# Attention and experts: normalizing the attention output in PSUM on VectorE, and all remainders on GpSimd

## The chip, the cores and the metric

The kernel runs on one core of a Trainium2 chip. TensorE (PE) does the matmuls into PSUM, VectorE (DVE), ScalarE (ACT) and GpSimd (POOL) do the elementwise work, and SyncE (SP) issues most of the DMAs. Each engine works through its own list of instructions in order and waits on semaphores for the others. The metric is the device time of one execution in microseconds (us); lower is better.

## The reference, cut to what matters

```python
scores = 1/sqrt(64) * q @ k.T                       # 8 batches, 8 heads, 576 positions, head size 64
bias   = minimum(-(cum[:, None] - cum[None, :]), 0) # cum = cumsum(maximum(s, 0))
scores = where(causal, -1e9, scores + bias)
attn   = exp(scores - max(scores))
attn   = attn / (sum(attn) + 1e-9)
x      = (attn @ v)                                 # heads side by side: 4608 tokens x 512
...
logits = x @ w_gate                                 # each of 8 experts takes 576 tokens
out[mask] = relu(x[mask] @ w1[e]) @ w2[e]
```

Matmuls are done in 16-bit pieces: a float32 number is the sum of a 16-bit "hi" piece and a "lo" piece, the remainder. So q, k, v, the exponentials P and the result x are each split, and the products of the pieces are added in PSUM.

## The kernel before

The program is one long hand-made schedule. Attention comes first, on 16 groups g of four heads (two groups make a batch); then come routing and the eight experts, which the change does not touch.

**The slots.** `run` (L600) walks through slots, 14 to a group; half a group (seven slots) belongs to one pair of heads, `pr`. In a slot the code first issues the slot's transposed score matmuls with their exponential (`st_units`, one unit a slot), then what earlier slots have posted (`post`, a number of slots later), then what the plan has for that slot. The table `T` (L39) holds the offsets. An engine's list is thus fixed by the order of the slots; nothing is moved at run time.

**The stages of one group.** Three groups are in flight at a time.

1. Preparation: `hi2` makes the hi pieces of q, k and v on ACT, `lo2` the lo pieces on DVE, two operations for each (L267). Behind each lo operation, and behind each row maximum, `pop` issues one more DVE operation from a list of waiting ones.
2. First pass (`spass_units`, L284): scores for the row maximum. Seven units to a half group, in the order one(0,3), one(0,2), comb, both(0), one(1,3), one(1,2), both(1). PE writes a bank `pss`, and one slot later DVE takes its maximum into `mr` (L297). The tag `pss` has three banks, and the small transpose `psm` (and the router's `psl` once a batch) takes its turn in the same three: because `psm` stands between one(1,3) and one(1,2), the bank of both(1) is the one that one(1,3) had, in the slot before.
3. Second pass (`st_units`, L374): transposed scores into `pst`, three banks; ACT takes the exponential into `P` (L391); the remainder `R` = P minus its upper 16 bits is a subtraction (L393) on POOL, or on DVE for the first block of each half and for the small last block (128 x 128).
4. Product with v (`pv_units`, L438): PE adds three products for each block into `po` (L457 to L459). The tag `po` has two banks, one for each `par`; a half group fills first par 0 and then par 1.
5. Normalizing (`norm`, L463): DVE adds a small number to the row sum (L470) and takes its reciprocal (L471). For three heads of four, five ACT operations then multiply out of PSUM into the float32 tile `xf` (L475), and for the fourth one DVE multiplication does (L479).
6. Pieces of x: `xh` (L484) makes the hi piece from `xf` on ACT in three operations a group, `xl` (L492) the lo piece on POOL in three operations. `xtr` and `xout` then transpose and store them by DMA, and `logits` (L510) multiplies them by the gate, 40 x 2 matmuls in slot 3 of every second group.

The last batch (groups 14 and 15) has its own ending, `tail` (L527).

Of the kernel before, what the change touches and what calls it, by code (L numbers as in the profile page):

```python
# [21 lines left out]
DM = 512  # L22
# [10 lines left out]
VS = 256.0  # L33
# [22 lines left out]
class Attention:  # L56
# [208 lines left out]
    def lo2(self, x, h, o, sc):  # L265
        def f(p):
            self.nc.vector.scalar_tensor_tensor(o[:, p], x[:, p], sc, h[:, p], op0=OP.mult, op1=OP.subtract)  # L267
            self.pop()
        return [lambda p=p: f(p) for p in range(2)]

    def vprep_units(self, g):
        st = self.st[g]
        V = self.pc.tile([128, 2, 9, 65], F16, name="V", bufs=3)
        Vl = self.pc.tile([128, 2, 9, 64], F16, name="Vl", bufs=3)
        st.update(V=V, Vl=Vl)
        return ([(0, lambda: self.nc.gpsimd.memset(V[:, :, :, 64:65], 1.0))] +
                list(zip(T["VHI"], self.hi2(st["rv"], V[:, :, :, 0:64], VS))) +
                list(zip(T["VLO"], self.lo2(st["rv"], V[:, :, :, 0:64], Vl, VS))))

    def q0(self, par, i):  # L280

# [92 lines left out]
    def st_units(self, g):  # L374

        nc, st = self.nc, self.st[g]
        Q, K = st["Q"], st["K"]
        units = []

        def mm(ps, c0, n, par, pr, ki, q0, diag=False):  # L380
            ks = slice(128 * ki, 128 * ki + 128)
            nc.tensor.matmul(ps[:, c0:c0 + n], K[0:70, 0, par, pr, ks], Q[0:70, 0, pr, par, q0:q0 + n],  # L382
                             start=True, stop=False)
            nc.tensor.matmul(ps[:, c0:c0 + n], K[:, 1, par, pr, ks], Q[:, 1, pr, par, q0:q0 + n],  # L384
                             start=False, stop=not diag)
            if diag:
                nc.tensor.matmul(ps[:, c0:c0 + 128], self.identb, self.mT, start=False, stop=True)

        def fin(ps, pr, c0, n, gp):
            P, R = st["P", pr], st["R", pr]  # L390
            nc.scalar.activation(P[:, c0:c0 + n], ps[:, :n], AF.Exp, scale=1.0 / YS)  # L391
            eng = nc.gpsimd if gp else nc.vector
            self.post(lambda: eng.tensor_tensor(R[:, c0:c0 + n], P[:, c0:c0 + n], strided_hi(P)[:, c0:c0 + n],  # L393
                                                op=OP.subtract), T["RT"][0 if gp else 1])

        def bank(pr, par, j):
            if par == 0 and j == 0:
                st["P", pr] = self.w.tile([128, P0 + 2 * PW], F32, name="P")
                st["R", pr] = self.w.tile([128, P0 + 2 * PW], F16, name="R")
            ps = self.ps_t.tile([128, 512], F32, name="pst")  # L400
            o, t = 64 * par, 0 if par else 512
            if j == 0:
                mm(ps, 0, 512, par, pr, 0, o, diag=True)
            elif j == 1:
                mm(ps, 0, 64, par, pr, 0, t)
                for ki, c0, n in ((1, 64, 384),):
                    mm(ps, c0, n, par, pr, ki, o + 128, diag=True)
                mm(ps, 448, 64, par, pr, 1, t)
            else:
                mm(ps, 0, 256, par, pr, 2, o + 256, diag=True)  # L410
                mm(ps, 256, 64, par, pr, 2, t)
                mm(ps, 320, 64, par, pr, 3, t)
                mm(ps, 384, 128, par, pr, 3, o + 384, diag=True)
            fin(ps, pr, P0 + par * PW + 512 * j, 512, (par, j) not in
                (T["RE"][pr] if g == 2 * self.nb - 1 else T["RD"]))

        def last(pr):


            ps = self.ps_t.tile([128, 512], F32, name="pst")  # L420
            nc.tensor.matmul(ps[:, 0:128], self.identb, self.mL, start=True, stop=False)
            for par in range(2):
                q0 = self.q0(par, 4)
                for a, n in ((0, 70), (1, 128)):
                    k0 = (2 * par + pr) * S + 512 - 64 * par
                    nc.tensor.matmul(ps[:, 64 * par:64 * par + 64],
                                     K[0:n, a].rearrange("p h r s -> p (h r s)")[:, k0:k0 + 128],
                                     Q[0:n, a, pr, par, q0:q0 + 64], start=False, stop=(par == a == 1))
            fin(ps, pr, 0, 128, False)

        for pr in range(2):
            for par in range(2):
                for j in range(3):
                    units.append(lambda pr=pr, par=par, j=j: bank(pr, par, j))
            units.append(lambda pr=pr: last(pr))
        return units

    def pv_units(self, g, pr):  # L438
        nc = self.nc
        b, hf = divmod(g, 2)  # L440
# [21 lines left out]

        def norm(par, po):  # L463
            h = pr * 2 + par
            if h == 0:
                self.xfs[g] = self.w.tile([128, 5, DM // 2], F32, name="xf")
            xf = self.xfs[g]
            den = self.w.tile([128, 5, 2], F32, name="den")
            self.chain(("n", g, pr, par),
                       lambda: nc.vector.tensor_scalar(den[:, :, 0:1], po[:, :, 64:65], EPS, None, op0=OP.add),  # L470
                       lambda: nc.vector.reciprocal(den[:, :, 1:2], den[:, :, 0:1]))  # L471
            if T["NE" if g == 2 * self.nb - 1 else "NA"][h]:
                self.post(lambda: self.drain(("n", g, pr, par)), T["NT"][1])
                for i in range(5):
                    self.post(lambda i=i: nc.scalar.activation(xf[:, i, 64 * h:64 * h + 64], po[:, i, 0:64], AF.Copy,  # L475
                                                               scale=den[:, i, 1:2]), T["NT"][1])
            else:
                self.chain(("n", g, pr, par),
                           lambda: nc.vector.tensor_mul(xf[:, :, 64 * h:64 * h + 64], po[:, :, 0:64],  # L479
                                                        den[:, :, 1:2].to_broadcast([128, 5, 64])))  # L480

        return [lambda par=par, i=i: tile_(par, i) for par in range(2) for i in range(5)]

    def xh(self, g, i):  # L484
        self.drain()
        b, hf = divmod(g, 2)
        if (hf, i) == (0, 0):
            self.xps[b] = self.w.tile([128, 5, 2, DM], F16, name="xp")
        o = slice(2 * i, min(2 * i + 2, 5))
        self.nc.scalar.activation(self.xps[b][:, o, 0, 256 * hf:256 * hf + 256], self.xfs[g][:, o], AF.Copy)  # L490

    def xl(self, g, i):  # L492
        b, hf = divmod(g, 2)
        xp, c = self.xps[b], slice(256 * hf, 256 * hf + 256)
        o = slice(2 * i, min(2 * i + 2, 5))
        self.nc.gpsimd.tensor_tensor(xp[:, o, 1, c], self.xfs[g][:, o], xp[:, o, 0, c], op=OP.subtract)

    def xout(self, b, i):
        nc, xp = self.nc, self.xps[b]
# [100 lines left out]
    def run(self):  # L600
# [7 lines left out]
        def at(n, f, *a):  # L608
            plan.setdefault(n, []).append((f, a))
# [16 lines left out]
        for g in range(ng):  # L626
            s0 = 14 * g
# [98 lines left out]
NT = 8 * S  # L726
# [692 lines left out]
```

## Time and profile before

| | |
|---|---|
| time, median of 3 runs (lowest, highest) | 866.54 us (864.54, 866.61) |
| the profiled execution | 858.84 us, of it 857.1 us from first to last instruction |
| PE busy | 761.5 us (89% of the span) |
| DVE busy | 613.0 us (72%) |
| POOL busy | 478.4 us (56%) |
| ACT busy | 387.0 us (45%) |
| mean granted TensorE clock | 0.942 |

The shares are means over two quite different stages. Attention fills about the first 345 us, the experts the rest. Only the windows of the profile, which give the busy time of each engine in a stretch, tell what limits a stage. In a row of the timeline the first number is the start in us from the span's start and the second the duration; a bracket at the end gives the engine's idle time ahead of that instruction and what ended it. On DVE, ACT and POOL an instruction often starts some 0.04 to 0.1 us before the one ahead of it has ended, so that the step from start to start is a little shorter than the duration.

### The profile page before, as it was taken

Reading aid. Unit: us, or ns where it says so; the run is one execution under the profiler, and the core shown is the slowest. Engines: PE = TensorE matmul, PEld = TensorE weight load, DVE = VectorE, ACT = ScalarE, POOL = GpSimd, SP = SyncE. Lnnn points to the kernel's source line nnn. Section 1 sums busy time; section 2 is a strip of 40 time slices with the busy share of each in tenths; the row PEclk is TensorE's granted clock in tenths of the full one; section 3 lists DMA queues with packets and bytes.
Section 4 is the critical chain, followed back from the end, with each engine's and each line's share of the span. In section 5 each row is a group of like instructions: output and inputs, shape, how many; then the busy total and the mean of one; then the engine's idle time right before and its main releaser. Section 6 shows DMA issues by size and latency. Waiting matters only on the chain.

```text
span 857.1 us, 22612 instructions
## 1 busy us (share of the span) xinstructions
PE 761.5 (89%) x9241; PEld 482.7 (56%) x9241; DVE 613.0 (72%) x1578; ACT 387.0 (45%) x866; POOL 478.4 (56%) x587
## 2 busy tenths in 40 slices
PE   8887899989889998269989999998989969959996
PEld 3576777877777787147545455454444525424442
DVE  6789999999999978668768878776677737115110
ACT  5466778878768787024213333231232113214110
POOL 5577899999989996062353534633462342432101
PEclk9689999999999999589999999999998979969999
DMA  6865999898988806052393837546283290491001
GB/s 176 249 178 151 198 238 236 207 236 234 232 205 223 177 31 141 33 187 67 114 188 103 223 101 194 151 134 169 81 211 107 95 221 28 125 210 62 31 13 43
DMA packets 122222, 128.69 MB, mean 150 GB/s; under 512 B 79781, under 2 KB 88329, under 8 KB 122118
## 3 DMA queue, kind: packets, MB, share of 16 engines
q1 hardware_dynamic: 103938, 74.31, 37.1%
q0 software_dynamic: 15744, 52.46, 20.3%
q8 instruction: 72, 1.18, 0.6%
q10 hardware_dynamic: 2436, 0.48, 0.3%
q14 instruction: 32, 0.26, 0.1%
HBM read 71.99 MB, written 19.49 MB: 107 GB/s over the span
## 4 chain that ended last, share of the span: by engine, by line
PE 48%; DVE 24%; issue 12%; DMA 5%; POOL 5%; ACT 3%; another core or an unknown queue 1%; ACTq 0%; SPq 0%; POOLq 0%; DVEq 0%
PE py L1146 15%; PE ph L1109 15%; DVE mr L297 7%; DVE R L393 3%; PE pht L1113 2%; PE py L1137 2%; DVE K L267 2%; DVE Vl L267 2%; PE ph L1111 2%; PE cnt L883 2%; POOL R L393 2%; PE pi L1013 1%; DVE Q L267 1%; DMA md<-mt 1%; DMA Q<-Q 1%
## 5 line engine op out<-in xcount | busy, mean ns | idle before, releaser
L393 POOL TENSOR_TENSOR R<-P 128x512 f16<-128x512 f32 x158 | 195.9, 1254 | 19.3 <-ACT P L391 19.3
L1109 PE MATMUL ph<-xT,w1p 128*128 128x512 f16 x696 | 187.1, 391 | 11.8 <-issue 11.7
L1146 PE MATMUL py<-w2p,hT 128*128 128x512 f16 x768 | 177.1, 381 | 0.3 <-issue 0.3
L1051 POOL DMA_INDIRECT wst<-in_w_dram,iw x96 | 98.3, 1024 | 138.8 <-DVE iw L857 40.4
L1113 PE MATMUL pht<-xT,w1p 128*128 128x64 f16 x768 | 139.0, 195 | 8.9 <-issue 8.7
L297 DVE TENSOR_REDUCE mr<-pss 128x1 f32<-128x512 f32 (+4 forms) x224 | 133.5, 608 | 9.9 <-PE pss L305 5.7
L391 ACT ACTIVATE P<-pst 128x512 f32<-128x512 f32 (+1 forms) x224 | 120.5, 563 | 41.4 <-PE pst L384 14.6
L1158 POOL DMA_INDIRECT out_dram<-y,ids x40 | 42.7, 1068 | 155.9 <-ACT y L1148 127.2
L1109 PEld LDWEIGHTS <-w1p 128*128 128x128 f16 x696 | 69.5, 100 | 93.8 <-issue 22.5
L1146 PEld LDWEIGHTS <-hT 128*128 128x128 f16 x768 | 70.2, 98 | 81.5 <-issue 5.4
L1117 ACT ACTIVATE hT<-ph 128x512 f16<-128x512 f32 x64 | 38.1, 597 | 169.5 <-PE ph L1109 89.0
L459 PE MATMUL po<-V,R 128*128 128x65 f16 x960 | 112.9, 195 | 1.3 <-POOL R L393 1.0
L457 PE MATMUL po<-V,P 128*128 128x65 f16 x960 | 112.4, 196 | 0.9 <-DVE xf L479 0.9
L458 PE MATMUL po<-Vl,P 128*128 128x64 f16 x960 | 112.3, 194 | 0.0
L382 PE MATMUL pst<-Q,K 70*128 70x64 f16 (+4 forms) x512 | 104.7, 253 | 4.3 <-ACT P L391 3.0
L384 PE MATMUL pst<-Q,K 128*128 128x64 f16 (+4 forms) x512 | 105.4, 253 | 0.0
L1126 DVE SCALAR_TENSOR_TENSOR hT<-ph,hT 128x512 f16<-128x512 f32 x64 | 43.8, 687 | 84.9 <-ACT hT L1117 54.4
L457 PEld LDWEIGHTS <-P 128*128 128x128 bf16 x960 | 91.1, 99 | 5.6 <-issue 0.2
L303 PE MATMUL pss<-K,Q 67*128 67x512 f16 (+3 forms) x256 | 72.5, 311 | 22.8 <-DVE mr L297 19.6
L459 PEld LDWEIGHTS <-R 128*128 128x128 f16 x960 | 90.3, 98 | 1.8 <-POOL R L393 1.5
L458 PEld LDWEIGHTS <-P 128*128 128x128 bf16 x960 | 90.2, 100 | 1.1 <-issue 1.0
L1113 PEld LDWEIGHTS <-w1p 128*128 128x128 f16 x768 | 71.3, 99 | 12.9 <-issue 12.2
(223 smaller groups left out, 1562.7 us busy)
## 6 DMA issues: line engine op xcount, KB each, us to landing
rq<-in_q_dram SPq DMA_DIRECT2D x32, 288.0 KB
rk<-in_k_dram SPq DMA_DIRECT2D x32, 288.0 KB
rv<-in_v_dram SPq DMA_DIRECT2D x32, 288.0 KB
Q<-Q SPq DMA_DIRECT2D x62, 144.0 KB
K<-K SPq DMA_DIRECT2D x62, 144.0 KB
xs<-xp SPq DMA_DIRECT2D x32, 256.0 KB
wst<-in_w_dram,iw POOLq DMA_INDIRECT x96
xs<-xp SPq DMA_DIRECT2D x8, 128.0 KB
```

Source lines behind the costliest of these rows:

```text
L297: nc.vector.tensor_reduce(o, ps, AX.X, OP.max)
L382: nc.tensor.matmul(ps[:, c0:c0 + n], K[0:70, 0, par, pr, ks], Q[0:70, 0, pr, par, q0:q0 + n], start=True, stop=False)
L384: nc.tensor.matmul(ps[:, c0:c0 + n], K[:, 1, par, pr, ks], Q[:, 1, pr, par, q0:q0 + n], start=False, stop=not diag)
L391: nc.scalar.activation(P[:, c0:c0 + n], ps[:, :n], AF.Exp, scale=1.0 / YS)
L393: self.post(lambda: eng.tensor_tensor(R[:, c0:c0 + n], P[:, c0:c0 + n], strided_hi(P)[:, c0:c0 + n], op=OP.subtract), T["RT"][0 if gp else 1])
L457: nc.tensor.matmul(po[:, i, :], H[:, c:c + 128], V[:, pr, sl, :], start=f, stop=False)
L458: nc.tensor.matmul(po[:, i, 0:64], H[:, c:c + 128], Vl[:, pr, sl, :], start=False, stop=False)
L459: nc.tensor.matmul(po[:, i, :], R[:, c:c + 128], V[:, pr, sl, :], start=False, stop=l)
L1051: nc.gpsimd.indirect_dma_start(out=t, out_offset=None, in_=src, in_offset=bass.IndirectOffsetOnAxis(ap=iw[:, k:k + 1], axis=0))
L1109: nc.tensor.matmul(ph, w, xT[:, 0:4, 4 * b + c], start=first, stop=last)
L1113: nc.tensor.matmul(pt[:, f], w, xT[:, 4, 4 * b + c, 0:64], start=first, stop=last)
L1146: nc.tensor.matmul(py, hT[:, f, a, 128 * i:128 * i + n], w2p[:, f, b], start=first, stop=last)
```

## The change

- `norm` multiplies on DVE for all heads, and for the first seven batches writes the product back into `po`, in PSUM, in place.
- The pieces are made from `po` a head at a time: one slot later ACT copies it to the hi piece, and one slot after that DVE subtracts and writes the lo piece (each 128 x 320). `xh`, `xl` and, for these batches, `xf` go. The bank of `po` is free only after that subtraction.
- The three DVE operations of a `norm` are now issued together, ahead of the other work posted for the slot (`drain`), where before they were popped one at a time behind other operations.
- All remainders `R` of groups 0 to 14 go to POOL (`RD=()`, and `last`); group 15 keeps its own split.
- v's lo piece is one DVE operation of 128 x 1152, where there were two of 128 x 576.
- In the last batch `xf` lies in the buffers of the raw v, and group 14's products, too, are made on DVE.

```diff
-T = dict(HI=(0, 1, 2, 2), LO=(2, 3, 5, 7), B=(3, 5, 8, 8, 10), VHI=(6, 8), VLO=(13, 11), RD=((0, 0),), RT=(3, 3),
-         XH=(23, 27, 24), XL=(26, 29, 34), XT=(27, 29, 30, 30, 36), LG=(33, 34, 38, 43, 45), M=(2, 5, 10), G=(-50,
-         -42, -26), V=(-17, -14), PV=(7, 7), NT=(1, 1), NA=(1, 1, 1, 0), RE=(((0, 0),
+T = dict(HI=(0, 1, 2, 2), LO=(2, 3, 5, 7), B=(3, 5, 8, 8, 10), VHI=(6, 8), VLO=(13,), RD=(), RT=(3, 3),
+         XT=(27, 29, 30, 30, 36), LG=(33, 34, 38, 43, 45), M=(2, 5, 10), G=(-50,
+         -42, -26), V=(-17, -14), PV=(7, 7), NT=(1, 1), NA=(0, 0, 0, 0), RE=(((0, 0),
...
-        return [lambda p=p: f(p) for p in range(2)]
+        return [lambda p=p: f(p) for p in (range(2) if halves else [slice(0, 2)])]
...
-            fin(ps, pr, 0, 128, False)
+            fin(ps, pr, 0, 128, g < 2 * self.nb - 1)
...
-            if h == 0:
-                self.xfs[g] = self.w.tile([128, 5, DM // 2], F32, name="xf")
-            xf = self.xfs[g]
+            end = g // 2 == self.nb - 1
+            if end and h == 0:
+                self.xfs[g] = self.raw.tile([128, 5, DM // 2], F32, name="xf", tag="rv")
+            if not end and (hf, h) == (0, 0):
+                self.xps[b] = self.w.tile([128, 5, 2, DM], F16, name="xp")
+
+            o = self.xfs[g][:, :, 64 * h:64 * h + 64] if end else po[:, :, 0:64]
...
-                self.chain(("n", g, pr, par),
-                           lambda: nc.vector.tensor_mul(xf[:, :, 64 * h:64 * h + 64], po[:, :, 0:64],
-                                                        den[:, :, 1:2].to_broadcast([128, 5, 64])))
+                self.chain(("n", g, pr, par), lambda: nc.vector.tensor_mul(
+                    o, po[:, :, 0:64], den[:, :, 1:2].to_broadcast([128, 5, 64])))
+            if not end:
+                xp, c = self.xps[b], slice(64 * (4 * hf + h), 64 * (4 * hf + h) + 64)
+
+                def pieces():
+                    nc.scalar.activation(xp[:, :, 0, c], o, AF.Copy)
+                    self.post(lambda: nc.vector.tensor_tensor(xp[:, :, 1, c], o, xp[:, :, 0, c], op=OP.subtract), 1)
+
+                self.drain(("n", g, pr, par))
+                self.post(pieces, T["NT"][1])
...
-                for i in range(3):
-                    at(s0 + T["XH"][i], self.xh, g, i)
-                    at(s0 + T["XL"][i], self.xl, g, i)
```

The list of DVE before, in the steady part of attention, from a half's maximum of one(1,3) to the next half's one(0,3). Rows with `mr` are maxima, `den` rows the normalizing, `R` rows the remainders, `K` a lo piece:

```order
L297 TENSOR_REDUCE mr_3006<-pss_3166 128x1
L470 TENSOR_SCALAR den_3178<-po_3051 128x5
L267 SCALAR_TENSOR_TENSOR K0_85<-rk_2655,K0_85 128x576
L471 RECIPROCAL den_3178<-den_3178 128x5
L297 TENSOR_REDUCE mr_3006<-pss_3187 128x1
L479 TENSOR_TENSOR xf_2793<-po_3051,den_3178 128x5x64
L393 TENSOR_TENSOR R_2918<-P_2917 128x128
L297 TENSOR_REDUCE mr_3006<-pss_3221 128x2
L393 TENSOR_TENSOR R_3171<-P_3170 128x512
L297 TENSOR_REDUCE mr_3253<-pss_3282 128x1
```

The same place in the changed kernel, from the maximum of one(1,3) on to the subtraction of the following par 0 (`xp<-po,xp` is the new lo piece, L482 the product in place):

```order
L297 TENSOR_REDUCE mr_2953<-pss_3110 128x1
L267 SCALAR_TENSOR_TENSOR K0_85<-rk_2610,K0_85 128x576
L297 TENSOR_REDUCE mr_2953<-pss_3132 128x1
L489 TENSOR_TENSOR xp_2749<-po_3000,xp_2749 128x5x64
L297 TENSOR_REDUCE mr_2953<-pss_3166 128x2
L474 TENSOR_SCALAR den_3235<-po_3136 128x5
L475 RECIPROCAL den_3235<-den_3235 128x5
L482 TENSOR_TENSOR po_3136<-po_3136,den_3235 128x5x64
L297 TENSOR_REDUCE mr_3197<-pss_3226 128x1
L297 TENSOR_REDUCE mr_3197<-pss_3246 128x1
L489 TENSOR_TENSOR xp_2749<-po_3136,xp_2749 128x5x64
```

Both remainders have left the list, the three operations of `norm` stand together, and the subtraction for par 0 stands two maxima behind its product.

The list of ACT in the changed kernel, around the hi piece of par 0 (`P<-pst` are the exponentials of three successive slots):

```order
L391 ACTIVATE P_4349<-pst_4461 128x512
L391 ACTIVATE P_4349<-pst_4523 128x512
L488 ACTIVATE xp_3748<-po_4371 128x5x64
L391 ACTIVATE P_4349<-pst_4558 128x512
L372 DMA Q1_82<-md_4367 2x2x576
L391 ACTIVATE P_4349<-pst_4597 128x128
```

The copy stands behind the exponential of its slot; where it stands there were five operations `xf<-po,den` before.

More of the change, by code (lines that the diff above doesn't have):

```diff
@@ L263, in hi2, with lo2 @@
         return [lambda p=p: self.nc.scalar.activation(o[:, p], x[:, p], AF.Copy, scale=sc) for p in range(2)]
-    def lo2(self, x, h, o, sc):
+    def lo2(self, x, h, o, sc, halves=True):
         def f(p):
@@ L277, in vprep_units @@
                 list(zip(T["VHI"], self.hi2(st["rv"], V[:, :, :, 0:64], VS))) +
-                list(zip(T["VLO"], self.lo2(st["rv"], V[:, :, :, 0:64], Vl, VS))))
+                list(zip(T["VLO"], self.lo2(st["rv"], V[:, :, :, 0:64], Vl, VS, False))))
     def q0(self, par, i):
@@ L474, in norm @@
                 for i in range(5):
-                    self.post(lambda i=i: nc.scalar.activation(xf[:, i, 64 * h:64 * h + 64], po[:, i, 0:64], AF.Copy,
+                    self.post(lambda i=i: nc.scalar.activation(o[:, i], po[:, i, 0:64], AF.Copy,
                                                                scale=den[:, i, 1:2]), T["NT"][1])
             else:
-                self.chain(("n", g, pr, par),
-                           lambda: nc.vector.tensor_mul(xf[:, :, 64 * h:64 * h + 64], po[:, :, 0:64],
-                                                        den[:, :, 1:2].to_broadcast([128, 5, 64])))
-        return [lambda par=par, i=i: tile_(par, i) for par in range(2) for i in range(5)]
[L484 to L496, printed above, removed]
+                self.chain(("n", g, pr, par), lambda: nc.vector.tensor_mul(
[7 more added lines that the diff above has]
+                self.post(pieces, T["NT"][1])
+        return [lambda par=par, i=i: tile_(par, i) for par in range(2) for i in range(5)]
     def xout(self, b, i):
```

## The prediction

> **What bounds the kernel now.** I read the windows first. In attention two engines are full at once, and PE is not:
>
> ```profile
> core 0: us, PE busy (x) PEld busy (x) DVE busy (x) ACT busy (x) POOL busy (x), PEclk, DMA share, GB/s
> 175.00:200.00 25.00, 23.15 (x467) 19.31 (x465) 24.86 (x48) 19.93 (x55) 24.29 (x28) 1.00 1.00 232
> 300.00:325.00 25.00, 23.82 (x512) 20.36 (x511) 18.13 (x38) 21.51 (x65) 24.53 (x27) 1.00 0.24 64
> ```
>
> DVE is busy 99.4% of 175 to 200 us and POOL 97%; from 300 us on, without preparation for later groups, DVE has room and PE sets the pace. The timeline gives the period. POOL's memset of `V` stands once in a group; between the two rows below stand ten more of them, so eleven periods take 206.87 us, 18.81 each:
>
> ```profile
> 99.26 0.17 POOL L276 MEMSET V<- 128x18 f16 x1
> 306.13 0.17 POOL L276 MEMSET V<- 128x18 f16 x1
> ```
>
> These eleven periods are where the change acts. An undisturbed one is 18.65 us (the small DVE remainder starts at 155.66 and, below, at 174.31); two hold popped router work as well. PE works 23.15/25 of it, 17.3 us.
>
> Why both are full is seen where they meet, first POOL and DVE in one stretch of the timeline, then the statistics of lines (ns, minimum/median/maximum):
>
> ```profile
> 155.33 1.04 POOL L393 TENSOR_TENSOR R<-P 128x512 f16<-128x512 f32 x1
> 155.66 0.85 DVE L393 TENSOR_TENSOR R<-P 128x128 f16<-128x128 f32 x1
> 156.33 1.21 POOL L496 TENSOR_TENSOR xp<-xf,xp 128x512 f16<-128x512 f32 x1
> L479 DVE TENSOR_TENSOR xf<-po,den x19: 474/476/492, 66.2 to 338.9; 128x320 f32<-128x320 f32 x19
> L393 POOL TENSOR_TENSOR R<-P x158: 1030/1100/1635, 33.5 to 334.6; 128x512 f16<-128x512 f32 x158
> L393 DVE TENSOR_TENSOR R<-P x66: 275/856/1531, 33.6 to 334.4; 128x512 f16<-128x512 f32 x34, 128x128 f16<-128x128 f32 x32
> L267 DVE SCALAR_TENSOR_TENSOR K<-rk,K x30: 739/926/1527, 12.4 to 279.6; 128x576 f16<-128x576 f32 x30
> ```
>
> A DVE operation with two inputs in SBUF and a POOL operation exclude each other: the 128x128 remainder, 0.275 at best, ends 0.14 after the POOL operation beside it has, and POOL's next one takes 0.17 more than its 1.04. With an input in PSUM (L479) DVE never waits. The Trainium skill, "SBUF — State Buffer", section "Who interferes with whom", states it as a rule: two-SBUF-input DVE operations and GpSimd's reads share a port pair under an exclusive lock, and one SBUF input does not contend. The trace agrees; followed alone, the rule makes this change a gain, and its sum is that of the first rival below.
>
> **The change, by DVE's sum.** Groups by shape over five periods (137.0 to 230.6):
>
> ```profile
> L393 DVE TENSOR_TENSOR R<-P 128x512 f16<-128x512 f32 x10 | 12.2, 1223 | 0.0
> L393 DVE TENSOR_TENSOR R<-P 128x128 f16<-128x128 f32 x10 | 5.7, 565 | 0.0
> L267 DVE SCALAR_TENSOR_TENSOR Vl<-rv,V 128x576 f16<-128x576 f32 x10 | 13.0, 1296 | 0.0
> L267 DVE SCALAR_TENSOR_TENSOR K<-rk,K 128x576 f16<-128x576 f32 x10 | 11.7, 1172 | 0.0
> L393 POOL TENSOR_TENSOR R<-P 128x512 f16<-128x512 f32 x51 | 63.4, 1257 | 0.3 <-ACT P L391 0.3
> L496 POOL TENSOR_TENSOR xp<-xf,xp 128x512 f16<-128x512 f32 x10 | 14.4, 1442 | 0.0
> L496 POOL TENSOR_TENSOR xp<-xf,xp 128x256 f16<-128x256 f32 x5 | 5.9, 1184 | 0.0
> ```
>
> A step is a duration less 0.08 of overlap. Out per group: four remainders, (12.2+5.7)/5 − 4×0.08 = 3.26. Two `Vl`, 2.44, become one: 0.74 for the first 576 columns, 0.60 for the next (from 0.275 at 128 to 0.74 at 576 is 1.04 ns a column), plus the 0.55 that one waits now (1.296−0.74), less 0.08: 1.81, so 0.63 out. In: four subtractions at L479's step, 0.40, make 1.6, bounded below by that row's 0.4 and above by 0.8 if PSUM with a 16-bit output is as slow as a contended row. Four norms, each a chain of dependent operations that now stands alone:
>
> ```profile
> 337.70 0.15 DVE L470 TENSOR_SCALAR den<-po 128x5 f32<-128x5 f32 x1
> 337.89 0.19 DVE L471 RECIPROCAL den<-den 128x5 f32<-128x5 f32 x1
> 338.11 0.49 DVE L479 TENSOR_TENSOR xf<-po,den 128x320 f32<-128x320 f32 x1
> ```
>
> That is 0.19+0.22+0.41 = 0.82, 3.28 for four; before, the first two cost at most 0.29 a head (rows below) and there was one product, 1.56. In: 1.72. Writing PSUM instead of SBUF isn't in the trace; I price it as L479, from 0.1 cheaper to 0.1 dearer each. Sum: 18.65 − 3.26 − 0.63 + 1.6 + 1.72 = 18.1.
>
> POOL loses three subtractions ((14.4+5.9)/5 = 4.06) and gets two large remainders (2 x 1.26) and two small ones. A remainder of 128 columns on POOL is not in the trace: between 0.26 (a quarter of the 1.04 at 155.33) and 1.05 (on the line through its 1.44 at 512 columns and 1.18 at 256); I take 0.5. POOL's sum falls by 0.5, or rises by as much at the upper bound. ACT loses 15 small products and three copies and gets four copies; it had room, so I count nothing.
>
> **The change, by the loop.** DVE's sum holds only if DVE never waits, and the new subtraction makes it wait. The rows of half a period:
>
> ```profile
> 172.99 0.68 DVE L297 TENSOR_REDUCE mr<-pss 128x1 f32<-128x512 f32 x1
> 173.59 0.15 DVE L470 TENSOR_SCALAR den<-po 128x5 f32<-128x5 f32 x1
> 173.77 0.19 DVE L471 RECIPROCAL den<-den 128x5 f32<-128x5 f32 x1
> 173.88 0.52 DVE L297 TENSOR_REDUCE mr<-pss 128x1 f32<-128x384 f32 x1
> 174.31 0.85 DVE L393 TENSOR_TENSOR R<-P 128x128 f16<-128x128 f32 x1
> 175.09 0.68 DVE L297 TENSOR_REDUCE mr<-pss 128x2 f32<-128x512 f32 x1
> 175.69 1.11 DVE L267 SCALAR_TENSOR_TENSOR Q<-rq,Q 128x576 f16<-128x576 f32 x1
> 176.72 1.52 DVE L393 TENSOR_TENSOR R<-P 128x512 f16<-128x512 f32 x1
> ...
> 172.08 0.22 PE L387 MATMUL pst<-mT,identb 128*128 128x128 bf16 x1
> 173.72 0.27 PE L303 MATMUL pss<-K,Q 67*128 67x256 f16 x1 [0.37 <-DVE mr L297]
> 177.29 0.19 PE L384 MATMUL pst<-Q,K 128*128 128x64 f16 x1
> ...
> 172.39 0.60 ACT L391 ACTIVATE P<-pst 128x512 f32<-128x512 f32 x1 [0.49 <-PE pst L387]
> ```
>
> The maximum of one(1,3) is done at 173.59 in steps; only then gets PE the bank for both(1), at 173.72. From there PE needs until 177.48, without a wait, for the score unit three slots on. ACT starts an exponential 0.09 after its matmul (172.30 to 172.39), so at 177.57; it takes 0.60, and the copy of par 0 stands behind it:
>
> ```profile
> L391 ACT ACTIVATE P<-pst 128x512 f32<-128x512 f32 x192 | 113.7, 606 | 31.8 <-PE pst L384 14.6 <-PE pst L387 8.1 <-DMA md<-mt 3.3
> L391 ACT ACTIVATE P<-pst 128x128 f32<-128x128 f32 x32 | 9.7, 302 | 9.7 <-PE pss L305 4.7 <-PE pst L426 2.2 <-DMA xt<-xp 1.1
> ```
>
> Between these shapes 320 columns out of PSUM are 0.45. So the subtraction can't start before 178.62: **5.03 us** after the maximum of one(1,3). DVE itself would be there sooner in the half that has one `K` ahead: 1.09 (`K` with its wait), 0.43, 0.40, 0.60, 0.82, 0.60, 0.43 = 4.37. In the other half, with two `Q`, it needs about as long as the loop. Behind the waiting subtraction stand all maxima, and PE waits for those banks.
>
> From the subtraction to the next half's maximum of one(1,3): 0.40, comb 0.52 (448 columns, between 0.43 and 0.60), both(0) with its small one 0.6, norm 0.82, the maximum 0.60, and `K` 1.09 in one half (4.03) or `Vl` 1.81 in the other (4.75). The gate's matmuls stand inside the 5.03 in every second group; their first row and the row behind them:
>
> ```profile
> 157.84 0.17 PE L516 MATMUL psl<-wgp,xt 128*128 128x16 f16 x1
> 158.85 0.19 PE L457 MATMUL po<-V,P 128*128 128x65 f16 x1
> ```
>
> 1.01 every second period is 0.5. **Sum: 2 x 5.03 + 4.03 + 4.75 + 0.5 = 19.34, against 18.65: +0.69 a period, +7.6 over eleven.** The two port waits that count in it (0.43 for `K`, 0.55 for `Vl`) are the unknown: at nothing the period is 18.36 (−3.2 in all), at a whole POOL operation of 1.0 each it is 20.4 (+19). I take today's means. In the two longer periods (11 x 0.16 = 1.8 in all) the router's operations fall into DVE's new waits; I take 1 back.
>
> In the last groups PE waits for POOL:
>
> ```profile
> PEld L459 <- POOL R L393: 1.5, 3, 1.0
> PE po L459 <- POOL R L393: 1.0, 2, 0.9
> ```
>
> POOL's subtractions of group 13 now stand among those remainders; without them up to 2.5 goes, and I take 1.5. Before 99 us DVE is less full (its sum is about even there) and I count nothing, within ±2. In all 7.6 − 1 − 1.5 = **+5.1 us**. The profiled execution took 858.84 (span 857.1 and 1.7 around it), 0.9% below the median of 866.54; its stages are those of the others, so I add to the median: **871.6**.
>
> **Rivals.** *The port decides, and it is faster.* If the copies are always there in time, DVE runs at its sum, 18.1: −0.55 x 11 − 1.5, about 859. For it speak the 3.26 us of contended remainders; against it the 5.03. It decides once the two halves' loops are 0.35 shorter each, or both port waits fall from 0.98 to under 0.29. *It comes out even:* waits about half of today's, 18.85 a period, 867. *PE sets the pace at 17.3:* −1.35 x 11 − 1.5, 850; DVE's sum speaks against it. *POOL's small last remainder is late:* PE needs it in the very slot in which it is issued, and it stands behind five large ones; one POOL operation late, 1.0, in one half lengthens the loop to 20.3, about 883. POOL's sum, below 18 of 19.3, speaks against it.
>
> **How the numbers follow.** Loop 0.47, late remainder 0.07: slower 0.54. Even 0.18. Port relief 0.22 and PE's pace 0.06: faster 0.28. About 0.3% (2.6 us) is what a measurement can tell from no change. The likeliest case alone reaches from 867 to 879. For 8 in 10 the range takes in most of the port rival, and port waits of some 0.9 each: 859.5 to 881; PE's pace, the late remainder and the rest of the port rival stay out.
>
> **What would show it.** Right: a period above 18.65 between `V` memsets; DVE below 97% busy with waits of 0.3 to 1.2 us at L489, put down to ACT's copy (L488), about one a group; POOL below 95%; no large PE wait for `R` from 300 us on. Wrong: no waits at L489 and DVE full; a product or subtraction far from 0.48; PE waiting for POOL's `R`.

## The result, and the profile after

| | before | after |
|---|---|---|
| time, median (lowest, highest) | 865.54 us (859.19, 866.61; 4 runs) | 889.33 us (887.34, 891.66; 4 runs) |
| ratio, 95% interval | 1 | 1.0298 (1.0268 to 1.0329) |
| profiled execution, its span | 858.84, 857.1 | 890.24, 888.5 |
| mean granted TensorE clock | 0.942 | 0.924 |
| PE, DVE, POOL, ACT busy | 761.5, 613.0, 478.4, 387.0 us | 776.7, 606.1, 465.4, 352.5 us |

The change makes the kernel slower by 23.8 us, where 5.1 were forecast. (The ratio compares the executions of both and is not the quotient of the two medians.) The windows of after that answer to those of before (columns as there):

```profile
175.00:200.00 25.00, 22.92 (x406) 18.77 (x405) 21.88 (x48) 15.83 (x32) 20.59 (x26) 0.93 0.92 224
300.00:325.00 25.00, 22.92 (x441) 19.16 (x440) 21.48 (x47) 14.72 (x32) 20.74 (x27) 1.00 0.75 183
```

In steady attention no engine is full any more: DVE 88% (99.4% before), POOL 82% (97%). So something waits in a circle. The DMA share is near 1 here as before, but from 104.4 to 328.7 us no wait of PE, DVE or POOL is put down to a DMA, and ACT's two come to 1.1 us. And the clock column, 1.00 there before, is 0.93. The fifth and the last memset of `V`, from the timeline of after:

```profile
104.44 0.18 POOL L276 MEMSET V<- 128x18 f16 x1
...
328.74 0.18 POOL L276 MEMSET V<- 128x18 f16 x1
```

Eleven periods take 224.3 us, against 206.87: +17.4. The two profiled spans differ by 31.4, more than the medians do, because the profiled execution of before was short (858.84, with a median of 865.54); so these parts can't be added up to the 23.8. They are 5.2 in the start (104.44 against 99.26), 17.4 in these periods, 4.1 from the last memset to the last product with v (36.0 against 31.9), and 4.7 in what follows, which the change doesn't touch (523.8 against 519.1) and which varies between profiles of other kernels here, too, from 516.6 to 523.9. Four of the eleven, by windows cut at the memsets:

```profile
146.30:166.60 20.30, 17.93 (x305) 14.63 (x302) 17.70 (x38) 12.59 (x25) 17.15 (x22) 0.92 1.01 253
...
166.63:186.49 19.86, 18.22 (x372) 15.24 (x370) 18.30 (x40) 13.03 (x27) 17.25 (x22) 1.00 0.61 170
...
206.90:228.30 21.40, 19.38 (x360) 16.02 (x357) 18.43 (x40) 12.87 (x27) 16.84 (x22) 0.92 0.58 163
...
228.33:247.19 18.86, 16.49 (x306) 13.39 (x303) 17.63 (x38) 12.47 (x25) 17.04 (x22) 1.00 1.03 242
```

Read the clock column beside the length. At clock 1.00 a period takes 18.86 without the gate's matmuls and 19.86 with them (PE's count of matmuls tells them apart, some 305 and 370): a mean of **19.36, where the prediction's loop gave 19.34**. At 0.92 each kind takes some 1.5 us more. Where the low clock comes from is seen a microsecond at a time, after PE's row just ahead of it:

```profile
128.68 0.27 PE L303 MATMUL pss<-K,Q 67*128 67x256 f16 x1 [1.79 <-DVE mr L297]
```

```profile
129.00:130.00 1.00, 1.00 (x21) 0.95 (x19) 1.00 (x3) 0.69 (x1) 0.46 (x1) 0.73 0.02 5
130.00:131.00 1.00, 1.00 (x20) 1.00 (x18) 0.75 (x2) 0.58 (x2) 0.76 (x2) 0.50 0.10 26
131.00:132.00 1.00, 1.00 (x17) 0.81 (x15) 0.10 (x1) 1.00 (x3) 0.92 (x3) 0.50 0.62 141
132.00:133.00 1.00, 1.00 (x5) 0.43 (x4) 0.93 (x4) 0.16 (x1) 0.42 (x1) 0.56 0.03 6
133.00:134.00 1.00, 1.00 (x41) 1.00 (x40) 1.00 (x2) 0.60 (x1) 0.10 (x1) 1.00 0.63 143
```

PE waits 1.79 us for the bank of both(1). Less than a microsecond later its clock is 0.50, from 129.46 (0.73 in that window is half of its last 0.54) to 132.88: 3.42 us. Such a time at 0.50 is called a half-clock stretch below. Between the two memsets after has five of them and one of twice the length, 23.9 us; at half clock that is worth up to 11.9 us of PE's work. The waits of the same stretch, 104.4 to 328.7 us, name that wait, and the one that was forecast (total, times, longest):

```profile
PE pss L303 <- DVE mr L297: 22.3, 22, 1.9
...
DVE xp L489 <- ACT xp L488: 10.7, 20, 1.1
```

Why the wait for both(1) is so long, DVE's rows show at another such place, then PE's:

```profile
145.78 0.56 DVE L297 TENSOR_REDUCE mr<-pss 128x3 f32<-128x384 f32 x1 [0.18 <-PE pss L330]
146.37 0.15 DVE L297 TENSOR_REDUCE mr<-mr 128x1 f32<-128x2 f32 x1
146.45 2.17 DVE L267 SCALAR_TENSOR_TENSOR Vl<-rv,V 128x1152 f16<-128x1152 f32 x1
148.54 0.15 DVE L474 TENSOR_SCALAR den<-po 128x5 f32<-128x5 f32 x1
148.73 0.19 DVE L475 RECIPROCAL den<-den 128x5 f32<-128x5 f32 x1
148.95 0.50 DVE L482 TENSOR_TENSOR po<-po,den 128x320 f32<-128x320 f32 x1
149.36 1.15 DVE L297 TENSOR_REDUCE mr<-pss 128x1 f32<-128x512 f32 x2
```

```profile
148.01 0.19 PE L384 MATMUL pst<-Q,K 128*128 128x64 f16 x1
150.10 0.37 PE L303 MATMUL pss<-K,Q 67*128 67x256 f16 x1 [1.89 <-DVE mr L297]
```

The merged `Vl`, 2.17 us, and the norm stand in one block ahead of the maximum of one(1,3), the first half of the row at 149.36; PE has nothing else to do and gets the bank when that is done. The row at 150.10 already runs at the low clock: 0.37 for 256 columns, where 128.68 shows 0.27.

### The profile page after: what moved, and what is told of

The parts are those of the page before. It is cut to its first block, busy times and chain, and to the rows that moved or that the text cites. A ratio compares the mean times of both kernels' runs of the same rounds, so it can differ in the third digit from the quotient of the medians.

```text
span 888.5 us, 22414 instructions
## 1 busy us (share of the span) xinstructions
PE 776.7 (87%) x9241; PEld 493.2 (56%) x9241; DVE 606.1 (68%) x1603; ACT 352.5 (40%) x655; POOL 465.4 (52%) x605
## 2 busy tenths in 40 slices
DMA packets 122221, 128.68 MB, mean 145 GB/s; under 512 B 79781, under 2 KB 88329, under 8 KB 122118
## 4 chain that ended last, share of the span: by engine, by line
PE 58%; DVE 16%; issue 10%; DMA 4%; ACT 4%; POOL 3%; another core or an unknown queue 2%; SPq 1%; ACTq 0%; POOLq 0%; DVEq 0%
PE ph L1104 14%; PE py L1141 14%; DVE mr L297 5%; PE pst L382 3%; PE pst L384 3%; PE pss L303 3%; DVE Vl L267 3%; PE py L1132 2%; PE pht L1108 2%; PE ph L1106 2%; PE po L457 2%; PE po L459 2%; PE po L458 2%; PE cnt L878 2%
## 5 line engine op out<-in xcount | busy, mean ns | idle before, releaser
L393 POOL TENSOR_TENSOR R<-P 128x512 f16<-128x512 f32 (+1 forms) x218 | 237.2, 1110 | 41.2 <-ACT P L391 40.6
L457 PE MATMUL po<-V,P 128*128 128x65 f16 x960 | 117.2, 200 | 1.2 <-DVE xf L482 1.2
L459 PE MATMUL po<-V,R 128*128 128x65 f16 x960 | 117.4, 198 | 0.7 <-POOL R L393 0.7
L458 PE MATMUL po<-Vl,P 128*128 128x64 f16 x960 | 117.0, 197 | 0.0
L382 PE MATMUL pst<-Q,K 70*128 70x64 f16 (+4 forms) x512 | 107.4, 259 | 0.7 <-ACT P L391 0.6
L384 PE MATMUL pst<-Q,K 128*128 128x64 f16 (+4 forms) x512 | 107.8, 257 | 0.0
L303 PE MATMUL pss<-K,Q 67*128 67x512 f16 (+3 forms) x256 | 74.5, 318 | 37.5 <-DVE mr L297 30.8
L457 PEld LDWEIGHTS <-P 128*128 128x128 bf16 x960 | 94.1, 101 | 6.4 <-issue 1.1
L458 PEld LDWEIGHTS <-P 128*128 128x128 bf16 x960 | 93.1, 103 | 1.3 <-issue 1.3
L459 PEld LDWEIGHTS <-R 128*128 128x128 f16 x960 | 93.2, 101 | 0.8 <-POOL R L393 0.8
```

The costliest lines, as they stand in the source:

```text
L303: nc.tensor.matmul(ps[:, :n], Q[0:67, 0, pr, par, q0:q0 + 128], K[0:67, 0, par, pr, 0:n], start=True, stop=False)
L457: nc.tensor.matmul(po[:, i, :], H[:, c:c + 128], V[:, pr, sl, :], start=f, stop=False)
L458: nc.tensor.matmul(po[:, i, 0:64], H[:, c:c + 128], Vl[:, pr, sl, :], start=False, stop=False)
L459: nc.tensor.matmul(po[:, i, :], R[:, c:c + 128], V[:, pr, sl, :], start=False, stop=l)
```

## The experiments

Three groups of runs, each on one chip: 1 to 4, 5 to 8, and 9 to 12. The median of before beside them was 865.53 (7 runs), 863.81 (13) and 862.75 (13); ratios are to before in the same group, with 95% intervals. A difference of two medians from different groups is less sure, by the 2 to 3 us by which these three differ; after itself ran beside the 865.54 above.

**1. PE kept busy ahead of the bank.** After, with 20 matmuls of 64 zero columns (`self.zz`, a tile that is set to zero once) added to `po` a little ahead of the wait:

```diff
+                if (pr, par, i, ki) == (1, 0, 1, 1):
+                    for _ in range(20):
+                        nc.tensor.matmul(po[:, i, 0:64], H[:, c:c + 128], self.zz, start=False, stop=False)
```

> The changed kernel with 20 more matmuls of 64 zero columns in each group, added into an open region of po (so the sums stay the same), just ahead of the place where PE waits some 1.85 us a period for the maximum of one(1,3). They are about 0.6 us of PE work that falls into idle time. CLOCK theory (PE's wait of 1.7 us or more inside one 3.4 us window makes the granted clock drop to half for the next 3.4 us, about 1.5 us each time): the wait shrinks to about 1.25 us, the granted clock stays at 1.00 from 110 to 330 us, the period between V memsets falls from 20.4 to 21.4 back to 18.9 to 19.9, and the time falls by 8 to 14 us, to 875 to 881. LOOP theory (the period is lengthened by the wait at the subtraction alone, the clock only follows): nothing gained, 887 to 896, since PE has more to do.

878.48 us, 1.0151 (1.0093 to 1.0209): 10.9 below after, by adding work. The rows of PE around the first wait, then the two memsets:

```profile
125.97 0.76 PE L463 MATMUL po<-zz,P 128*128 128x64 f16 x20
...
128.14 0.27 PE L305 MATMUL pss<-K,Q 67*128 67x256 f16 x1 [0.87 <-DVE mr L299]
```

```profile
103.96 0.18 POOL L278 MEMSET V<- 128x18 f16 x1
...
319.49 0.18 POOL L278 MEMSET V<- 128x18 f16 x1
```

The wait is 0.87 where it was 1.79, one half-clock stretch is left between the memsets (108.0 to 111.4), and the eleven periods take 215.5, 8.8 less. Six windows of 3.41 us at half clock are gone (after has seven), which is 1.5 each, as the periods of after showed. No work was taken out of the kernel, and the periods at full clock take what after's own do, 18.9 to 19.9: the low clock is a cause, not a symptom.

**2. The copy earlier.** After, with ACT's copy in the slot of its product, the subtraction where it was:

```diff
-                def pieces():
...
-                self.post(pieces, T["NT"][1])
+                nc.scalar.activation(xp[:, :, 0, c], o, AF.Copy)
+                self.post(lambda: nc.vector.tensor_tensor(xp[:, :, 1, c], o, xp[:, :, 0, c], op=OP.subtract), 2)
```

> The changed kernel with ACT's copy issued in the slot of its norm, ahead of the next exponential, where it stood behind it; the subtraction keeps its place in DVE's list. LOOP and CLOCK theories together: the copy is there about 1 us sooner, waits at L489 fall from 20 us to under 5 us in all, the period goes to DVE's own sum of about 18 us, PE's longest wait falls below 1.6 us and the granted clock stays at 1.00: 852 to 866 us. LOOP without CLOCK as its consequence (the drops come whatever PE waits): 0.7 to 1.2 us less in each of eleven periods, 876 to 882. If neither: no change, waits move elsewhere, 886 to 892.

881.90, 1.0162 (1.0094 to 1.0231). L489's waits go, and ACT waits for the product instead, ahead of the exponentials; waits from 100 to 330 us:

```profile
PE pss L303 <- DVE mr L297: 25.6, 22, 1.9
...
ACT xp L488 <- DVE po L482: 20.6, 17, 2.6
```

The bank's wait is no shorter, and in the profile, the slowest of its executions (885.48), the eleven periods take 223.5, 0.8 less than in after. A wait moved is not a wait removed. The median lies where the second of the three theories put it, but the 0.7 to 1.2 a period that it gave as the reason are not there; what made the median fall by 7 is open.

**3. Before, made slower on DVE.** The maximum of both(0) is taken twice in one half of each group, 0.47 us more for DVE.

```diff
-                nc.vector.tensor_reduce(o, ps, AX.X, OP.max)
+                for _ in range(times):
+                    nc.vector.tensor_reduce(o, ps, AX.X, OP.max)
...
-            red(mrt[:, 0:a, i], ps[:, :a * n].rearrange("p (a n) -> p a n", a=a))
+            red(mrt[:, 0:a, i], ps[:, :a * n].rearrange("p (a n) -> p a n", a=a),
+                2 if i == 0 and pr == 0 else 1)
```

> The kernel before, with the maximum of both(0) taken twice in one half of each group (0.47 us more on DVE a period, same result), right ahead of the place where PE waits 1.46 us in every second period. LINEAR theory (the time follows DVE's sum): 0.47 x 13 to 15 groups, 6 to 7 us more than before, 871 to 873, clock 1.00 between 100 and 230 us. CLOCK theory: the wait grows beyond 1.6 us, four to eight drops of the granted clock appear in that stretch at 1 to 1.5 us each, and the time is 10 to 17 us more than before, 876 to 883.

877.53, 1.0153 (1.0091 to 1.0216), with four half-clock stretches between the memsets. It looks like the clock theory's answer; experiment 5 takes that back.

**4. The subtraction of par 0 a slot later.**

```diff
-                    self.post(lambda: nc.vector.tensor_tensor(xp[:, :, 1, c], o, xp[:, :, 0, c], op=OP.subtract), 1)
+                    self.post(lambda: nc.vector.tensor_tensor(xp[:, :, 1, c], o, xp[:, :, 0, c], op=OP.subtract), 2 - par)
```

> The changed kernel with the subtraction of par 0 one slot later in DVE's list. LOOP and CLOCK: the waits at L489 fall from 20 us to under 8 us, the period to 18 to 19 us, and with PE's wait below 1.6 us the clock stays at 1.00: 858 to 872 us. LOOP alone: 878 to 884. RIVAL (the bank of po comes free too late, and PE waits for DVE at L457 instead): no gain, 886 to 895, with waits of L457 or L303 on L489.

885.03, 1.0211 (1.0149 to 1.0273). One undisturbed period is 18.37, but the bank's waits of 1.3 to 1.95 stay, and five half-clock stretches with them. L489's waits fall to one of 0.8, yet the eleven periods take 222.0 (224.3 in after): the time lies between the bands of "loop alone" and of the rival, and no wait at L457 for DVE is seen.

**5. The slowed kernel of 3, PE kept busy.**

```diff
+                if (pr, par, i, ki) == (1, 1, 4, 2):
+                    for _ in range(30):
+                        nc.tensor.matmul(po[:, i, 0:64], H[:, c:c + 128], self.zz, start=False, stop=False)
```

> The slowed kernel of before (one maximum taken twice, 0.47 more on DVE in a period) with 30 matmuls of 64 zero columns ahead of the score bank that PE waits for, so that PE never idles for 1.6 us there; the output is the same. Clock theory (of the 12 us that the doubled maximum cost, 5.2 are the work and the rest the half clock after PE's long waits): the half-clock stretches between 100 and 300 us go, 869 to 873 us. Rival (the 12 us are the work itself and what it shifts): as the doubled maximum alone, 876 to 879, or more by the time of the added matmuls.

876.36, 1.0145 (1.0065 to 1.0225): no gain. PE's row at the same wait, first of 3, then of 5:

```profile
150.70 0.34 PE L304 MATMUL pss<-K,Q 67*128 67x384 f16 x1 [2.06 <-DVE mr L298]
```

```profile
151.87 0.34 PE L306 MATMUL pss<-K,Q 67*128 67x384 f16 x1 [1.24 <-DVE mr L300]
```

The waits shrink and three of the four stretches go, yet the eleven periods fall by only 2.5 (213.6 against 216.1), and the median by nothing that can be told. In the profile of 3, its fastest execution (869.94), periods of 20.2, 19.4 and 18.9 take turns, and the stretch of 152.2 to 155.6 lies in one of 18.9; in 5 most are 19.41. Over the first seven periods the mean is 19.60 in 3, with three stretches, and 19.42 in 5, with none. So here the low clock cost little, 0.2 a period. That PE catches up where DVE's list sets the pace, and can't where PE and DVE wait for each other, as in after, would explain both; no run tests it. The clock theory's number for 5 missed, and 3 is no evidence for it.

**6 to 9. The parts of the change, alone and taken back.** Before with all remainders on POOL (6); after with `Vl` in two operations again (7); after with the remainders back on DVE (8); before with the pieces from PSUM alone (9: as 8, with `Vl` in two).

```diff
@@ 6, in before @@
-VLO=(13, 11), RD=((0, 0),)
+VLO=(13, 11), RD=()
-            fin(ps, pr, 0, 128, False)
+            fin(ps, pr, 0, 128, g < 2 * self.nb - 1)
@@ 7, in after @@
-VLO=(13,)
+VLO=(13, 11)
-Vl, VS, False))))
+Vl, VS))))
@@ 8, in after @@
-VLO=(13,), RD=()
+VLO=(13,), RD=((0, 0),)
-            fin(ps, pr, 0, 128, g < 2 * self.nb - 1)
+            fin(ps, pr, 0, 128, False)
```

> One part of the change alone: before, with all remainders R of groups 0 to 14 on GpSimd, and nothing else changed. Theory (the remainders are the part that relieves DVE, but POOL at 97% of its time has no room for them unless its three subtractions for xp go too): POOL gets 2 x 1.26 + 2 x 0.5 more a group, the period becomes POOL's, about 21 us, 885 to 895 us. Rival (the port decides: POOL's operations become shorter without DVE's in the way, and DVE runs at 15.4): 852 to 862.

> One part of the change undone: after, with v's lo piece in two operations again. Theory (the loop sets the period, and PE's wait ahead of both(1) sets the clock): where one operation of 1.8 stood at once between the halves, the first operation goes to another slot, the half with Vl gets shorter by some 0.4, the wait of PE in that half comes below 1.6 us in part of the groups, and with it some of the half-clock stretches go: 876 to 884 us. Rival (the merged operation only saves a start and costs nothing): as after or up to 4 us slower, 886 to 893.

> Another part undone: after, with the remainders of each half's first block and small last block on DVE again, as before. Theory (a loop in which DVE's own operations stand in a chain): 3.26 more a group on DVE, of which the waits at L489 (1.2 a group) and DVE's waits for PE hide some: 890 to 905 us, waits at L489 mostly gone. Rival (DVE has room enough now, and POOL's operations are what is late): 878 to 888.

> Another part of the change alone: before, with the normalizing in PSUM and the pieces of x made from there, remainders and v's lo piece as before. Theory (the new chain of norm, copy and subtraction on DVE, with DVE's sum 18.65 - 3.28/... as in the prediction: nothing goes, 1.6 and 1.7 come, less the port waits that POOL's missing subtractions took from it): a period of 19.6 to 20.3, hardly any half-clock stretch, since the wait ahead of both(1) stays near 1.2: 876 to 888 us. Rival (POOL, freed of 4.06 a group, lets DVE's contended operations go so fast that it comes out near before): 862 to 870.

**10. The merged `Vl` alone, in before.**

> The third part alone: before, with v's lo piece in one operation. Theory (before is bound by DVE's sum, so the 0.63 that the merger saves counts, while PE's longer wait ahead of both(1) brings half-clock stretches that DVE's list partly hides, as in the kernel with the doubled maximum): 858 to 866 us, periods of 18.2 to 18.8 and PE's wait near 2 us in every second half. Rival (the merger costs here what it costs in after, some 16): 876 to 882 us.

| remainders on POOL | pieces from PSUM | `Vl` merged | median us | ratio, 95% interval |
|---|---|---|---|---|
| yes | | | 890.64 (6) | 1.0291 (1.0231 to 1.0350) |
| | | yes | 866.41 (10) | 1.0048 (1.0025 to 1.0071) |
| | yes | | 898.11 (9) | 1.0413 (1.0369 to 1.0458) |
| | yes | yes | 891.23 (8) | 1.0303 (1.0240 to 1.0366) |
| yes | yes | | **871.36** (7) | 1.0092 (1.0058 to 1.0126) |
| yes | yes | yes | 889.33 (after) | 1.0298 (1.0268 to 1.0329) |

(Remainders and `Vl` without the pieces were not tried.) One steady period each, of before and then of 6, 7, 8, 9 and 10, in windows from memset to memset:

```profile
155.26:173.91 18.65, 17.89 (x357) 14.84 (x356) 18.51 (x39) 15.37 (x41) 18.18 (x21) 1.00 0.83 214
```

```profile
163.43:184.11 20.68, 18.37 (x318) 14.96 (x316) 13.97 (x29) 13.06 (x34) 18.69 (x25) 0.83 0.63 178
```

```profile
162.12:180.87 18.75, 17.53 (x354) 14.63 (x352) 18.00 (x41) 12.78 (x27) 16.76 (x22) 1.00 0.85 222
```

```profile
168.69:188.97 20.28, 17.94 (x355) 14.84 (x354) 19.94 (x44) 12.66 (x26) 14.19 (x19) 1.00 0.65 181
```

```profile
170.31:191.74 21.43, 19.22 (x373) 15.59 (x370) 21.09 (x45) 12.89 (x27) 13.74 (x19) 1.00 0.57 162
```

```profile
158.87:177.61 18.74, 17.90 (x357) 14.84 (x356) 17.79 (x38) 15.41 (x41) 18.27 (x21) 1.00 0.81 222
```

6 and 8 came out in the bands that their theories gave. In 9 and 8 DVE is 98% full and the clock in these windows is 1.00. There the merger pays, and more than the 0.63 a group that the prediction priced: without it the two `Vl` take 1.280 each, merged the one takes 1.515, so some 0.97 a group is saved (with 0.08 of overlap taken off each operation), and the windows above differ by 1.15. The medians differ by 6.9 (898.11 to 891.23, from two groups), the ratios by 1.1%, the profiled eleven periods by 11.6. (For 9, 876 to 888 were expected, with hardly any half-clock stretch; there are three between its memsets, and the prediction's own sum for a list that only gains, 18.65 + 1.6 + 1.72 = 21.97, lay nearer to the 21.0 to 21.4 measured.) In 10 it takes 0.72 from DVE's busy time and the period doesn't fall: POOL is still busy 18.27 of 18.74. Neither expectation for 10 held: its time is not below before's (0.5% above it), PE's longest wait in the steady periods is 1.47 as in before, and there is no loss of 16. In after, where DVE waits anyway, it costs 18.0 (871.36 to 889.33). The expectation for 7 was too small, and DVE's rows of 7 show why:

```profile
178.28 0.75 DVE L267 SCALAR_TENSOR_TENSOR Vl<-rv,V 128x576 f16<-128x576 f32 x1
178.95 0.48 DVE L489 TENSOR_TENSOR xp<-po,xp 128x320 f16<-128x320 f32 x1
179.35 1.08 DVE L297 TENSOR_REDUCE mr<-pss 128x1 f32<-128x448 f32 x2
180.46 0.15 DVE L297 TENSOR_REDUCE mr<-mr 128x1 f32<-128x2 f32 x1
180.53 1.01 DVE L267 SCALAR_TENSOR_TENSOR Vl<-rv,V 128x576 f16<-128x576 f32 x1
```

```profile
183.02 0.27 PE L303 MATMUL pss<-K,Q 67*128 67x256 f16 x1 [0.79 <-DVE mr L297]
```

The first half stands ahead of the subtraction, in the time in which DVE would wait for ACT's copy, and is free; only the second stands ahead of the norm. The loop is shorter by what left it: 18.75 against 19.36, which is 6.7 over eleven periods. PE's wait falls from 1.89 to 0.79, and from 112 to 252 us there is no half-clock stretch. The 6.7 and experiment 1's 10.9 add up to about the 18.0; that the two parts are these is argued from the sum, not tested by a run.

In 6 DVE has far too little to do (13.97 of 20.68) and PE waits for POOL, from 104 to 325 us:

```profile
PEld L459 <- POOL R L393: 20.4, 14, 2.4
PE po L459 <- POOL R L393: 18.7, 14, 2.3
```

These waits bring half-clock stretches too (clock 0.83 in the window above); how the 27 us divide between POOL and the clock was not separated. The remainders need the pieces (4.06 us off POOL), and the pieces need the remainders off DVE: alone they cost 27 and 35, together 7.6.

**11. Both edits of 4 and 7. 12. Edit 7, with PE kept busy in groups 0 and 1** (8 of the zero matmuls in each tile of `po`):

```diff
@@ 12 @@
+                if g < 2 and l:
+                    for _ in range(8):
+                        nc.tensor.matmul(po[:, i, 0:64], H[:, c:c + 128], self.zz, start=False, stop=False)
```

> Two edits of after together: v's lo piece in two operations, and the subtraction of par 0 one slot later. Theory (each takes its own wait out of the loop, 0.6 and 0.5 a period where nothing else disturbs): the loop falls below DVE's own sum, undisturbed periods of 18.2 to 18.4, 863 to 868 us. Rival (with two operations DVE is full already, and the later subtraction only moves the wait to the bank po): as with the two operations alone, 869 to 874 us.

> After with v's lo piece in two operations and, for groups 0 and 1 alone, 8 matmuls of 64 zero columns added to every tile of po (the output is the same). Theory (the 5 us that the start is longer come from two stretches of half clock, at 58 to 65 and 71 to 78 us, that PE's waits bring about there): these stretches go or get shorter, the fifth memset of V stands at 101 to 102 instead of 104.2, and the time falls by 2 to 3, to 868 to 870 us. Rival (the start is longer because the new chain of norm, copy and subtraction stands on its path): the memset stays at 104 or comes later, 871 to 875 us.

871.89 (1.0112, 1.0072 to 1.0151) and 872.72 (1.0135, 1.0070 to 1.0201): both as 7, so the rivals' numbers. In 11 the later subtraction takes a steady period without the gate down to between 18.3 and 18.8, but two of three with it take 19.8, where 7 has some 18.75 for both. In 12 the start does what was expected. 72 to 78 us of 7, then of 12:

```profile
72.00:78.00 6.00, 6.00 (x66) 4.82 (x65) 2.69 (x8) 1.64 (x4) 1.45 (x3) 0.50 0.65 182
```

```profile
72.00:78.00 6.00, 6.00 (x134) 5.19 (x131) 5.12 (x12) 3.07 (x6) 2.69 (x3) 1.00 0.60 178
```

The stretch is gone and the fifth memset stands at 100.58 instead of 104.21. But 11, without these matmuls, has it at 100.77 in its profile, and experiment 1 at 103.96 without that stretch; and the median of 12 shows no gain. What the start costs in the mean of executions stays open. No version beat before.

## Why the prediction was right, and where it was wrong

The sign and the loop were right; the sum was 18.7 too small, because it has no term for the low clock, which takes some 10 of the 23.8 us.

- **The prices held.** Groups of after by shape, from 104.4 to 328.7 us:

```profile
L482 DVE TENSOR_TENSOR po<-po,den 128x320 f32<-128x320 f32 x44 | 22.0, 500 | 1.5
...
L393 POOL TENSOR_TENSOR R<-P 128x128 f16<-128x128 f32 x22 | 21.6, 980 | 0.0
...
L267 DVE SCALAR_TENSOR_TENSOR Vl<-rv,V 128x1152 f16<-128x1152 f32 x11 | 21.5, 1958 | 0.0
...
L489 DVE TENSOR_TENSOR xp<-po,xp 128x320 f16<-128x320 f32 x44 | 21.3, 485 | 10.7 <-ACT xp L488 10.7
```

  The product in place is 0.500, the subtraction 0.485 (priced near 0.48), the merged `Vl` 1.96, so 1.88 as a step, where 1.81 was taken. POOL's small remainder is 0.98: inside the bounds of 0.26 and 1.05, at their upper end and not at the 0.5 taken. No wait of PE for POOL's `R` is seen in these periods, and POOL has room.
- **The loop held.** 19.36 against 19.34, and its signs: L489 waits for L488 (20 times in eleven groups, up to 1.1 us), DVE 88%, POOL 82%. Around the period of 18.86, where no gate work stands, the two ways from the maximum of one(1,3) to the subtraction take 4.90 and 4.88 us, by the step 0.60 of a maximum, where 5.03 was predicted; the ways back take 4.13 and 4.96, for 4.03 and 4.75. So the parts hold within 0.2, and that the sum hits to 0.02 is luck. One of the two subtractions waits, as the prediction had it for the half with one `K`:

```profile
245.91 0.49 DVE L489 TENSOR_TENSOR xp<-po,xp 128x320 f16<-128x320 f32 x1 [0.57 <-ACT xp L488]
```

  Over eleven periods the loop is 19.36 x 11 − 206.87 = 6.1, where 7.6 − 1 were predicted. The rival in which the port decides fell with it: DVE's sum of 18.1 is reached in no steady period of after, nor of 7 (18.4 to 18.9).
- **The step that failed** stands behind the loop: eleven periods at the rate of an undisturbed one. The working has "From there PE needs until 177.48, without a wait", which held at full clock, but the sum has no term for a lower clock; it was put at nothing without a reason. The loop makes PE wait longer for both(1), 1.79 to 1.89 us in six of the eleven halves with the merged `Vl`, and at four of these waits the clock fell for 3.4 us. It fell twice more, at 109.0 after a wait of 2.33 for ACT, and at 262.6 for 6.8 us, around two waits of 1.3 and 1.4 in the period that holds the router's work. What the low clock cost in the periods is at most 17.4 − 6.1 = 11.3, in which the router's work stands too; experiment 1 took 8.8 of that away with one stretch of some 1.5 left, so about 10. The sum also took the merger for a small gain on DVE and a term of the loop; in after, with the others in place, it is 18.0 of the 23.8.
- **A sign of it stood in the trace of before**, unread. PE's rows of its two waits near 240 us, then the clock a microsecond at a time:

```profile
240.56 0.32 PE L303 MATMUL pss<-K,Q 67*128 67x384 f16 x1 [2.03 <-DVE mr L297]
...
242.30 0.27 PE L303 MATMUL pss<-K,Q 67*128 67x256 f16 x1 [0.57 <-DVE mr L297]
```

```profile
242.00:243.00 1.00, 0.70 (x14) 0.67 (x14) 1.00 (x4) 0.65 (x3) 0.56 (x1) 1.00 0.00 0
243.00:244.00 1.00, 1.00 (x15) 0.92 (x12) 1.00 (x4) 0.54 (x1) 0.88 (x1) 0.50 0.11 21
244.00:245.00 1.00, 1.00 (x22) 1.00 (x21) 1.00 (x5) 0.88 (x2) 0.20 (x1) 0.50 0.62 141
```

  Its usual waits there, 1.35 to 1.47 us, leave the clock alone. Here the 3.41 us ahead of the low clock, 239.59 to 243.00, hold 0.97 of the first wait and all 0.57 of the second, 1.55 in sum by unrounded times.
- **Start and ending.** Nothing within ±2 was counted for the start, and −1.5 for the last groups; the profiles show +5.2 and +4.1. Of PE's waits for POOL's `R` in the last groups one is left, of 0.8 (three before, 1.5 in all), but the stretch is longer all the same (34.2 in 7, 36.7 in experiment 1, 31.9 before). Neither cause was settled.
- **The bound of before** was read as DVE alone. Experiment 10 shows that DVE's list could lose 0.72 without any gain: POOL, or the loop through both, was as late.

## What to carry to other kernels

Price an operation by the place at which it stands, not by its busy time: the same merger saved 7 to 12 us where its engine was full, nothing where another engine was as late, and cost 18 where it stood ahead of the maximum that frees PE's next bank. When a change lengthens a wait of PE, compare the new wait with those in the trace that did and did not bring the granted clock down, and add what the low clock costs to the sum. And try the parts of a change alone: here two parts that cost 27 and 35 us alone came to 7.6 together, and the third, which looked like a detail, was most of the loss.

## What the runs showed of the hardware

The granted clock steps in windows of 3.41 us on a grid that runs on through the whole execution. In the fourteen profiles of this case, from about 105 to 320 us, no window at full clock in which PE idled at most 1.47 us in sum was followed by one at half clock; all with more than 1.75 were; between 1.50 and 1.75 both occur. (PE's idle time is taken between the ends that the profile models.) So where a wait lies on the grid counts: in after, a wait of 1.89 us from 148.21 on put 1.74 into the window that ends at 149.95, and the clock fell; one of the same length from 230.24 on put 1.63 into the window that ends at 231.87 and 0.26 into the next, and it did not. One window at half clock costs some 1.5 us in after (20.34 against 18.86, 21.42 against 19.86), and less in experiment 3.

The Trainium skill, "TensorE: Matmul & The Clock Gate", Part 1 (the HAM clock gate), states half rate after at least one idle window of about 3.4 us, on a free-running window. The trace agrees on the window (3.41 us), the grid and the half rate (0.50); if an idle window is one without any work, it does not agree on the idle time: some 1.8 us of 3.41 were enough here, and the measurement decides.
